# One ordered transfer queue and residues formed by TensorE in a retention + gMLP kernel

## The chip, the cores and the metric

The kernel runs on one core of a Trainium2 chip, as one launch. The metric is the device time in microseconds of one execution; runs are given by their median. Inside a profile, times count from the first instruction, and the span is what lies between the first and the last. PE is TensorE, DVE is VectorE, ACT is ScalarE, POOL is GpSimd, SP is SyncE. "ACT's queue" and "SP's queue" are the DMA queues on which these two engines issue transfers.

## The reference

Two stages on float32 inputs. Retention: batch 4, 8 heads, 768 positions, head width 64, with a state per head that decays by `gamma`. Its output `x` (4, 768, 512) goes through a gated MLP with a matmul over the positions:

```python
for t in range(S):
    state = gamma[None, :, None, None] * state + np.einsum('bhd,bhe->bhde', k[:, :, t], v[:, :, t])
    y[:, :, t] = scale * np.einsum('bhd,bhde->bhe', q[:, :, t], state)
...
h = np.maximum(x @ w_in, 0.0)                      # 512 -> 1024
u, v = (h[..., :d_ff // 2], h[..., d_ff // 2:])
mu = np.mean(v, axis=-1, keepdims=True)
var = np.mean((v - mu) ** 2, axis=-1, keepdims=True)
v_n = (v - mu) / np.sqrt(var + 1e-06)
v_s = np.einsum('ts,bsd->btd', w_spatial, v_n) + b_spatial[None, :, None]   # 768 x 768
gated = u * v_s
return (gated @ w_out).astype(np.float32)          # 512 -> 512
```

The four weights arrive as float64 (`w_in`, `w_out`) or float32 (`w_spatial`).

## The kernel before

**Pairs.** TensorE's fast type here is `F32R`. To keep float32 accuracy, each operand of the MLP is kept as a pair, a high part (a cast to `F32R`) and a low part (the residue, whole minus high), and a product is three matmuls (`split3`, through `mm` at L110): high x high, high x low, low x high. Low parts are made by `residue` (L118), a subtraction on VectorE or POOL. The products of retention are plain float32.

**Retention.** 24 groups of 128 positions, six to a batch. `load_group(g)` brings `qv` (two transfers of 256 KB), `kk` (512 KB) and `qd` (256 KB) on SP's queue (L115), and POOL multiplies the two halves of the values in `qv` by a decay (L214). `ret_set(g)` makes scores for group g+1 and the update of the state of group g: 32 + 32 small matmuls, called `s`, whose results VectorE adds to the state (L250) or masks (L257). `ret_out(g)` makes `x`: 16 matmuls on PE, a multiplication by `qd` on VectorE into `xf` (L283), a cast on ACT into `xh` (L286) and a residue on POOL into `xl`.

**MLP.** `mlp_v(b, c)` is 12 matmuls into `v`, relu on ACT into `vr` (L320), statistics on VectorE (L321, L322) and three tiny steps on POOL that give `rs` and `nb` (L323 to L326). `mlp_norm` normalises on ACT (L332), casts to `vnh` (L333) and forms `vnl`. `item(b, i)` is one of eight pieces to a batch: `u` (12 matmuls, relu into `ur` at L354), `sp`, the spatial matmul (18 matmuls), the gate on VectorE, ACT and POOL, and `o`, 9 matmuls with `w_out`.

**Weights.** `w_in` (its v half as `winv`, its u half as `winu`) and `w_out` come as 12 raw blocks of 512 KB. `load_double(i)` loads one; `split_double(i)` makes the pair from the words of the float64: absolute value on ACT (L154), five integer and scaling steps on VectorE (L155 to L159) that leave the float32 value in `df` and a small rest in `da`, a cast on ACT into the high part (L160), the residue `df` minus high, and an addition of `da` on POOL that stores the low part (L162). The residue of blocks 0 to 3 is on VectorE, of the others on POOL. `load_spatial` brings the spatial weight in pieces (`wst`), and `split_spatial(c, half)` makes a 128 x 384 pair: a cast on ACT (L187) and a residue, 11 of 12 on VectorE, one on POOL. Raw blocks, the spatial weight and the bias `b_sp` all go on ACT's queue.

**Order.** The program text is written as words: S, X, G, L, C (split_double), K (load_spatial), W (split_spatial), V, N, I, O as above, U and Z for `ret_set` without scores or without the update. Four strings hold them: START (everything of batch 0 up to its norms), FIRST (items of batch 0 beside retention of batch 1), REST and LAST. From this text a scheduler sets the order of the instructions on each engine, by its own estimate of time; transfers keep the order of the text, and so do matmuls behind START (`pinned`). Each engine then runs its own list strictly in order, and so does each queue's issuer: an instruction that waits for a semaphore holds all that are behind it. Tiles come from pools with a number of buffers; a transfer into a buffer waits until the last reader of what was in it is done. `qv`, `kk` and `qd` have 3 buffers each, raw blocks from the sixth on have 2.

Of the kernel before, what the change touches and what calls it, by code (L numbers as in the profile page):

```python
# [26 lines left out]


START = (
    "v m L0 G0 L1 L2 L3 G1 C0 C1 S-1 G2 L4 L5 C2 S0 X0 C3 S1 X1 G3 V0 C4 S2 X2 V1 C5 G4 K0 S3 X3 "  # L30
    "N0 V2 K2 N1 V3 G5 S4 X4 N2 K4 K5 V4 N3 B U5 X5 N4 V5 L6 L7 W00 W10 W20 N5 W30 W40 W50"
)
FIRST = (
    "C6 I0 G6 C7 L8 W01 C8 L9 I1 G7 W11 W21 Z5 C9 L10 I2 S6 W31 G8 C10 L11 I3 X6 S7 W41 W51 G9 C11 "
    "I4 X7 S8 G10 I5 X8 S9 G11 I6 X9 S10 G12 V0 V1 I7 X10 S11 N0 V2 N1 V3 N2 G13 X11 V4 N3 V5 N4 O7 "
    "N5"
)
# [4 lines left out]
LAST = "I0 I1 I2 I3 I4 I5 I6 I7 O7"  # L42


BLOCKS = [0, 1, 2, 3, 4, 5, 6, 8, 7, 9, 10, 11]
VECTOR_BLOCKS = 4
VECTOR_SPATIAL = 11
WARM_UP = 10
QD_BUFS = 3


@with_exitstack
def tile_retention_gmlp(
# [7 lines left out]
    w_out: bass.AP,  # L61
    b_sp: bass.AP,
    mask: bass.AP,
    vdecay: bass.AP,
    qdecay: bass.AP,
    out: bass.AP,
):
    nc = tc.nc
    P = 128
    B = out.shape[0]  # L70
    NG = kk.shape[0]
    NC = NG // B
# [12 lines left out]
    wpool = ctx.enter_context(tc.tile_pool(name="weights", bufs=1))  # L85
    rpool = ctx.enter_context(tc.tile_pool(name="ret", bufs=2))
    mpool = ctx.enter_context(tc.tile_pool(name="mlp", bufs=2))
    ps_r = ctx.enter_context(tc.tile_pool(name="ps_r", bufs=3, space=bass.MemoryType.PSUM))
    ps_m = ctx.enter_context(tc.tile_pool(name="ps_m", bufs=2, space=bass.MemoryType.PSUM))
    ps_o = ctx.enter_context(tc.tile_pool(name="ps_o", bufs=3, space=bass.MemoryType.PSUM))  # L90

    mask_t = wpool.tile([P, C], F32, name="mask_t")
    vd_t = wpool.tile([P, NC, 2, NP], F32, name="vd_t")
    bsp_t = wpool.tile([P, S], F32, name="bsp_t")
    mhalf = wpool.tile([P, 1], F32, name="mhalf")
# [6 lines left out]
    wsp_h = wpool.tile([P, NC, S], F32R, name="wsp_h")  # L102
    wsp_l = wpool.tile([P, NC, S], F32R, name="wsp_l")
# [5 lines left out]
    def mm(out, lhs, rhs, start, stop, pin=False):  # L109
        ins = nc.tensor.matmul(out, lhs, rhs, start=start, stop=stop)  # L110
        if pin or pinned:
            tc.keep_in_program_order(ins)

    def load(dst, src):
        tc.keep_in_program_order(nc.sync.dma_start(dst, src))  # L115

    def residue(eng, out, whole, high):
        eng.tensor_tensor(out, whole, high.bitcast(F32), ALU.subtract)  # L118

    def pick(on_vector):  # L120
        return nc.vector if on_vector else nc.gpsimd

    doubles = [
        (w[:, k, 0], w[:, k, 1], src[:, k])
        for w, src in ((winv_w, w_inv), (winu_w, w_inu), (wout_w, w_out))
        for k in range(KT)
    ]
    doubles = [doubles[i] for i in BLOCKS]
    raws = {}

    def load_weight(dst, src):
        tc.keep_in_program_order(nc.scalar.dma_start(dst, src))

    def load_double(i):

        if i >= len(doubles):
            return
        if i < 6:
            tag = ("vnh", "vnl")[i // 3]
            if i % 3 == 0:  # L140
                raws[tag] = mpool.tile([P, 3, DM], I64, tag=tag, name=f"raw{i}", bufs=1)
            raws[i] = raws[tag][:, i % 3]
        else:
            raws[i] = mpool.tile([P, DM], I64, tag="raw", name=f"raw{i}")[:, :]
        load_weight(raws[i], doubles[i][2])

    def split_double(i):
        hi, lo, _ = doubles[i]
        parts = raws.pop(i).bitcast(I32).rearrange("p (n w) -> p n w", w=2)
        low, top = parts[:, :, 0], parts[:, :, 1]  # L150
        a = rpool.tile([P, DM], F32, tag="xf", name=f"da{i}")
        f = mpool.tile([P, DM], F32, tag="u", name=f"df{i}", bufs=3)
        ai, fi = a[:, :].bitcast(I32), f[:, :].bitcast(I32)
        nc.scalar.activation(a, top.bitcast(F32), AF.Abs)  # L154
# [7 lines left out]
        nc.gpsimd.tensor_tensor(lo, f, a, ALU.add)  # L162

    staged = {}

    def load_spatial(c):


        if c < 4:
            if c % 2 == 0:  # L170
                tag = ("xh", "xl")[c // 2]
                t = mpool.tile([P, 2, S], F32, tag=tag, name=f"wst{c}", bufs=3)
                load_weight(t, w_sp[:, c : c + 2])
                for i in range(2):
                    for half in range(2):
                        staged[c + i, half] = t[:, i, half * HALF : half * HALF + HALF]
        elif c < NC:
            for half in range(2):
                tag = ("t", "gh" if half else "gl")[c - 4]
                t = mpool.tile([P, HALF], F32, tag=tag, name=f"wst{c}_{half}")  # L180
                load_weight(t, w_sp[:, c, half * HALF : half * HALF + HALF])
                staged[c, half] = t[:, :]

    def split_spatial(c, half):
        cols = slice(half * HALF, half * HALF + HALF)
        whole = staged.pop((c, half))
        nc.scalar.copy(wsp_h[:, c, cols], whole)  # L187
        residue(pick(c + NC * half < VECTOR_SPATIAL), wsp_l[:, c, cols], whole, wsp_h[:, c, cols])

    queries = {}  # L190
    keys = {}
# [5 lines left out]
    def load_group(g):  # L197
        if g >= NG:
            return

        t = rpool.tile([P, 4, 2, NP, C], F32, tag="qv", name=f"qv{g}", bufs=3)
        kt = rpool.tile([P, 2, 2, NP, C], F32, tag="kk", name=f"kk{g}", bufs=3)
        qd = rpool.tile([P, NP, P], F32, tag="qd", name=f"qd{g}", bufs=QD_BUFS)
        for r in range(2):
            rows = t[ROWS[r], 2 * r : 2 * r + 2]
            load(rows.rearrange("p s i h c -> p (s i h c)"), qv[g, r])
        load(kt[:, :, :, :, :].rearrange("p s i h c -> p (s i h c)"), kk[g])
        load(qd, qdecay[g % NC])
        queries[g], keys[g], naturals[g] = (t[:, 2], t[:, 1]), kt[:, 0], kt[:, 1]
        values[g], decays[g] = (t[:, 0], t[:, 3]), qd  # L210
        for r in range(2):
            vd = vd_t[ROWS[r], g % NC].unsqueeze(3).broadcast_to([D, 2, NP, D])
            w = values[g][r][ROWS[r]]
            nc.gpsimd.tensor_tensor(w, w, vd, ALU.mult)  # L214
# [114 lines left out]
    def mlp_norm(b, c):  # L329
        vh, vl = vn[b]  # L330
        v, nb, rs = norm.pop((b, c))
        nc.scalar.activation(v, v, AF.Identity, bias=nb, scale=rs)  # L332
        nc.scalar.copy(vh[:, c], v)  # L333
        residue(nc.vector, vl[:, c], v, vh[:, c])

    gate = {}
    us = {}
# [72 lines left out]
    def item(b, i):  # L410
# [23 lines left out]
        "v": lambda b, g, n: load(vd_t, vdecay),  # L434
        "B": lambda b, g, n: load_weight(bsp_t, b_sp),
    }

    def emit(text, b, g0):
# [85 lines left out]
```

## Time and profile before

| | |
|---|---|
| median of 3 runs | 439.87 us (438.54 to 441.08) |
| profiled execution | 439.42 us |
| its span | 437.6 us |
| mean granted TensorE clock | 0.938 |
| PE busy | 383.7 us, 88% of the span |
| VectorE, POOL, ACT busy | 218.2, 174.7, 128.7 us |
| transfers | 47.44 MB in all; SP's queue 37.81 MB, ACT's 9.05 MB |

The profile's rows read as follows. A row of a timeline is: start, duration, engine, line, operation, written tile <- read tiles, shape, and in brackets how long the engine stood idle before it and what released it. A group of instructions is: count, then busy time, mean of one in ns, then idle time of the engine just before them. A row of waits is: who waited for whom, us in total, how many times, the longest. Several matmuls in one row overlap, so a single duration there is a little longer than its share. A float32 matmul stands as two records, an `F32R` matmul as one.

### The profile page before, as it was taken

The numbers are of one execution on the slowest core, as the hardware profiler recorded it, in microseconds if no ns is written. First come the engines' busy times: TensorE is split into PE (matmuls) and PEld (weight loads), VectorE is DVE, ScalarE is ACT, GpSimd is POOL, SyncE is SP. The second block draws the span as 40 slices with busy tenths as digits, with TensorE's granted clock in tenths as the row PEclk, the third lists the DMA queues.
The fourth block names the chain that finished last, engine by engine and source line by source line (L and its number), as shares of the span: only waits on it lengthen the run. The fifth ranks groups of instructions, "written<-read, shape, count | busy, mean of one in ns | idle before, by whom it ended". The sixth has DMA issues, their size and how long they took to land.

```text
span 437.6 us, 9093 instructions
## 1 busy us (share of the span) xinstructions
PE 383.7 (88%) x3786; PEld 338.0 (77%) x3786; DVE 218.2 (50%) x420; ACT 128.7 (29%) x231; POOL 174.7 (40%) x201
## 2 busy tenths in 40 slices
PE   3278964888897999999995799999999999999996
PEld 1156652787786988799994788898999988999995
DVE  4699995468775555455552223354554124322122
ACT  3122534433222114542112013451113124511212
POOL 1666765564544444634442222424352223211110
PEclk8588686889998999999999799999999999999999
DMA  8974659511244542164434500064441000100102
GB/s 245 284 246 122 195 191 272 173 48 54 94 121 124 158 154 61 63 193 121 146 99 148 166 0 1 0 191 124 124 121 73 0 1 0 73 0 1 73 0 73
DMA packets 17417, 47.44 MB, mean 108 GB/s; under 512 B 2528, under 2 KB 3296, under 8 KB 17376
## 3 DMA queue, kind: packets, MB, share of 16 engines
q1 hardware_dynamic: 14640, 37.81, 28.6%
q10 hardware_dynamic: 2736, 9.05, 6.7%
q8 instruction: 30, 0.49, 0.5%
q14 instruction: 11, 0.09, 0.1%
HBM read 40.56 MB, written 6.29 MB: 107 GB/s over the span
## 4 chain that ended last, share of the span: by engine, by line
PE 75%; DMA 9%; DVE 7%; POOL 3%; issue 2%; ACT 2%; SPq 1%; POOLq 0%; DVEq 0%; ACTq 0%
PE sp L110 21%; PE v L110 15%; PE o L110 14%; PE u L110 14%; PE s L110 6%; PE x L110 5%; DMA qv<-in_qv_dram 3%; DMA qd<-in_qdecay_dram 2%; DMA raw<-in_w_inu_dram 2%; DVE qv L257 1%; DMA kk<-in_kk_dram 1%; DVE df L157 1%; DMA raw<-in_w_out_dram 1%; POOL xl L118 1%; DVE qv L250 1%
## 5 line engine op out<-in xcount | busy, mean ns | idle before, releaser
L214 POOL TENSOR_TENSOR qv<-qv,vd_t 64x512 f32<-64x512 f32 x48 | 54.3, 1132 | 57.1 <-DMA qv<-in_qv_dram 49.8
L118 POOL TENSOR_TENSOR gl<-t,gh 128x384 fp32r<-128x384 f32 x31 | 31.5, 1016 | 111.5 <-ACT gh L380 110.4
L110 PE MATMUL u<-xh,winu_w 128*128 128x384 f32 x256 | 72.6, 347 | 1.9 <-POOL winu_w L162 1.9
L110 PE MATMUL sp<-wsp_h,vnh 128*128 128x384 f32 x192 | 64.9, 338 | 3.2 <-ACT ur L354 3.2
L110 PE MATMUL v<-winv_w,xh 128*128 128x512 f32 x192 | 65.4, 423 | 0.9 <-POOL winv_w L162 0.7
L110 PE MATMUL o<-wout_w,gh 128*128 128x512 f32 x192 | 61.1, 398 | 5.0 <-POOL wout_w L162 5.0
L110 PE MATMUL sp<-wsp_h,vnl 128*128 128x384 f32 x192 | 64.9, 338 | 0.0
L110 PE MATMUL sp<-wsp_l,vnh 128*128 128x384 f32 x192 | 64.9, 338 | 0.0
L378 DVE TENSOR_TENSOR t<-sp,bsp_t 128x384 f32<-128x384 f32 (+1 forms) x34 | 18.0, 534 | 90.9 <-PE sp L110 90.8
L110 PEld LDWEIGHTS u<-xh,winu_w 128*128 128x128 f32 x256 | 47.3, 190 | 3.9 <-POOL winu_w L162 2.3
L110 PE MATMUL s<-qv,kk 64*64 64x64 f32 x1440 | 31.5, 233 | 17.6 <-DMA kk<-in_kk_dram 13.2
L110 PEld LDWEIGHTS v<-winv_w,xh 128*128 128x128 f32 x192 | 38.8, 206 | 9.8 <-POOL winv_w L162 0.8
L110 PE MATMUL v<-winv_w,xl 128*128 128x512 f32 x96 | 40.7, 424 | 5.7 <-POOL xl L118 5.7
L110 PEld LDWEIGHTS o<-wout_w,gh 128*128 128x128 f32 x192 | 36.0, 189 | 11.6 <-POOL wout_w L162 5.8
L110 PEld LDWEIGHTS s<-qv,kk 64*64 64x64 f32 x1440 | 27.7, 144 | 21.5 <-issue 19.4
L380 ACT CAST gh<-t 128x384 fp32r<-128x384 f32 (+1 forms) x34 | 16.6, 493 | 92.5 <-DVE t L379 90.1
L257 DVE TENSOR_TENSOR qv<-s,mask_t 64x256 f32<-64x256 f32 x92 | 38.6, 420 | 10.1 <-PE s L110 8.7
L110 PE MATMUL u<-xl,winu_w 128*128 128x384 f32 x128 | 43.3, 338 | 0.0
L118 POOL TENSOR_TENSOR xl<-xf,xh 128x512 fp32r<-128x512 f32 x24 | 31.3, 1303 | 29.7 <-ACT xh L286 29.7
L110 PEld LDWEIGHTS x<-qv 128*64 128x64 f32 (+1 forms) x768 | 27.9, 146 | 16.5 <-DVE qv L250 8.3
L110 PEld LDWEIGHTS sp<-wsp_h,vnh 128*128 128x128 f32 x192 | 36.6, 191 | 3.6 <-ACT ur L354 3.5
L110 PE MATMUL x<-qv 128*64 128x64 f32 (+1 forms) x768 | 32.9, 236 | 6.4 <-DVE qv L250 6.1
(57 smaller groups left out, 525.9 us busy)
## 6 DMA issues: line engine op xcount, KB each, us to landing
qv<-in_qv_dram SPq DMA_DIRECT2D x48, 256.0 KB, 4.3
kk<-in_kk_dram SPq DMA_DIRECT2D x24, 512.0 KB, 5.6
qd<-in_qdecay_dram SPq DMA_DIRECT2D x24, 256.0 KB, 5.5
out_dram<-ot SPq DMA_DIRECT2D x23, 256.0 KB, 2.0
raw<-in_w_inv_dram ACTq DMA_DIRECT2D x4, 512.0 KB, 6.9
raw<-in_w_inu_dram ACTq DMA_DIRECT2D x4, 512.0 KB, 7.0
raw<-in_w_out_dram ACTq DMA_DIRECT2D x4, 512.0 KB, 3.8
wst<-in_w_sp_dram ACTq DMA_DIRECT2D x2, 768.0 KB, 6.2
```

Of the source, the lines that this page charges most:

```text
L110: ins = nc.tensor.matmul(out, lhs, rhs, start=start, stop=stop)
L118: eng.tensor_tensor(out, whole, high.bitcast(F32), ALU.subtract)
L157: nc.vector.scalar_tensor_tensor(fi, top, -0x40000000, ai, ALU.bitwise_and, ALU.bitwise_or)
L214: nc.gpsimd.tensor_tensor(w, w, vd, ALU.mult)
L250: nc.vector.tensor_tensor(dst, u, w[r][ROWS[1 - r], i], ALU.add)
L257: nc.vector.tensor_tensor(m[r][ROWS[r], i], ts[i][col, 0], mk, ALU.mult)
L378: nc.vector.tensor_tensor(t[:, c], pp[:, c], bsp_t[:, tc_], ALU.add)
L380: nc.scalar.copy(gh[:, c], t[:, c])
```

## The change

Four things change.

1. The raw blocks 0 to 8, the spatial weight, the bias and a new 128 x 128 float32 unit matrix `eye` go on SP's queue, in one order with the groups. Only blocks 9 to 11 stay on ACT's queue.
2. A new function `residue_unit` forms a residue on PE: one or two matmuls with the unit matrix in float32 put the whole into PSUM (for a weight block, `df` and `da`, which replaces POOL's addition too), one `F32R` matmul with minus the unit matrix takes the high part off, and ACT copies the result out of PSUM as the low part. It is used for blocks 0 to 3, six of the 12 spatial pieces and the six norm tiles of batch 0. The other six spatial residues are all on VectorE.
3. Raw blocks get 3 buffers instead of 2; `kk` and `qd` get 2 instead of 3.
4. START and FIRST are written in another order, so that group 6 and block 8 are loaded within START.

```diff
 START = (
-    "v m L0 G0 L1 L2 L3 G1 C0 C1 S-1 G2 L4 L5 C2 S0 X0 C3 S1 X1 G3 V0 C4 S2 X2 V1 C5 G4 K0 S3 X3 "
-    "N0 V2 K2 N1 V3 G5 S4 X4 N2 K4 K5 V4 N3 B U5 X5 N4 V5 L6 L7 W00 W10 W20 N5 W30 W40 W50"
+    "v m e L0 G0 C0 L1 L2 S-1 C1 G1 L3 C2 S0 X0 G2 C3 L4 L5 S1 X1 K0 V0 C4 G3 S2 X2 K2 V1 C5 N0 G4 L6 "
+    "S3 X3 V2 N1 G5 W00 W10 K4 K5 S4 X4 V3 N2 W20 W30 B V4 N3 L7 U5 X5 W40 W50 N4 V5 G6 N5 L8"
 )
 FIRST = (
-    "C6 I0 G6 C7 L8 W01 C8 L9 I1 G7 W11 W21 Z5 C9 L10 I2 S6 W31 G8 C10 L11 I3 X6 S7 W41 W51 G9 C11 "
+    "C6 L9 I0 C7 W01 L10 C8 I1 G7 W11 W21 Z5 L11 C9 I2 S6 W31 G8 C10 I3 X6 S7 W41 W51 G9 C11 "
     "I4 X7 S8 G10 I5 X8 S9 G11 I6 X9 S10 G12 V0 V1 I7 X10 S11 N0 V2 N1 V3 N2 G13 X11 V4 N3 V5 N4 O7 "
     "N5"
 )
...
-VECTOR_BLOCKS = 4
-VECTOR_SPATIAL = 11
+FIRST_QUEUE = 9
+UNIT_BLOCKS = 4
+UNIT_SPATIAL = 6
+UNIT_NORM = 6
+RAW_BUFS = 3
+KK_BUFS = 2
 WARM_UP = 10
-QD_BUFS = 3
+QD_BUFS = 2
...
+    def load_eye():
+        load(eye_t, eye)
+        nc.scalar.mul(minus_t, eye_t, -1.0)
+
+    def residue_unit(out, high, name, *parts):
+
+        n = out.shape[-1]
+        ps = ps_o.tile([P, DM], F32, tag="o", name=f"ru{name}")
+        for k, part in enumerate(parts):
+            mm(ps[:, :n], eye_t, part, start=(k == 0), stop=False)
+        mm(ps[:, :n], minus_t, high, start=False, stop=True)
+        nc.scalar.copy(out, ps[:, :n])
...
-            raws[i] = mpool.tile([P, DM], I64, tag="raw", name=f"raw{i}")[:, :]
-        load_weight(raws[i], doubles[i][2])
+            raws[i] = mpool.tile([P, DM], I64, tag="raw", name=f"raw{i}", bufs=RAW_BUFS)[:, :]
+        (load if i < FIRST_QUEUE else load_weight)(raws[i], doubles[i][2])
...
-        residue(pick(i < VECTOR_BLOCKS), f, f, hi)
-        nc.gpsimd.tensor_tensor(lo, f, a, ALU.add)
+        if i < UNIT_BLOCKS:
+            residue_unit(lo, hi, f"d{i}", f, a)
+        else:
+            residue(nc.gpsimd, f, f, hi)
+            nc.gpsimd.tensor_tensor(lo, f, a, ALU.add)
...
-                load_weight(t, w_sp[:, c : c + 2])
+                load(t, w_sp[:, c : c + 2])
...
-        residue(pick(c + NC * half < VECTOR_SPATIAL), wsp_l[:, c, cols], whole, wsp_h[:, c, cols])
+        if c + NC * half < UNIT_SPATIAL:
+            residue_unit(wsp_l[:, c, cols], wsp_h[:, c, cols], f"w{c}_{half}", whole)
+        else:
+            residue(nc.vector, wsp_l[:, c, cols], whole, wsp_h[:, c, cols])
...
-        kt = rpool.tile([P, 2, 2, NP, C], F32, tag="kk", name=f"kk{g}", bufs=3)
+        kt = rpool.tile([P, 2, 2, NP, C], F32, tag="kk", name=f"kk{g}", bufs=KK_BUFS)
...
-        residue(nc.vector, vl[:, c], v, vh[:, c])
+        if b * NC + c < UNIT_NORM:
+            residue_unit(vl[:, c], vh[:, c], f"n{b}_{c}", v)
+        else:
+            residue(nc.vector, vl[:, c], v, vh[:, c])
```

The scheduler gives the engines new orders in START. In the listings below, a row is line, operation, written tile <- read tiles, shape; numbers behind a tile's name count tiles. `raw3` is the buffer of blocks 3 to 5, `wst0` the first half of the spatial weight.

On SP, from the group 2 loads on. Before:

```order
L115 DMA qv2_166<-in_qv_dram 64x1024 x2
L115 DMA kk2_167<-in_kk_dram 128x1024
L115 DMA qd2_168<-in_qdecay_dram 128x512
L115 DMA qv3_327<-in_qv_dram 64x1024 x2
L115 DMA kk3_328<-in_kk_dram 128x1024
L115 DMA qd3_329<-in_qdecay_dram 128x512
```

After:

```order
L123 DMA qv2_255<-in_qv_dram 64x1024 x2
L123 DMA kk2_256<-in_kk_dram 128x1024
L123 DMA qd2_257<-in_qdecay_dram 128x512
L123 DMA raw3_174<-in_w_inu_dram 128x512 x2
L123 DMA wst0_343<-in_w_sp_dram 128x1536
L123 DMA qv3_382<-in_qv_dram 64x1024 x2
L123 DMA kk3_383<-in_kk_dram 128x1024
L123 DMA qd3_384<-in_qdecay_dram 128x512
L123 DMA wst2_454<-in_w_sp_dram 128x1536
L123 DMA qv4_497<-in_qv_dram 64x1024 x2
```

Weight blocks 4 and 5 and the spatial weight now stand between the groups, behind `qd2` and `qd3`; `qd2` goes into the buffer that `qd0` had, `qd3` into that of `qd1`.

On VectorE, around `xf1`, the last step of group 1's `x`. Before:

```order
L257 TENSOR_TENSOR qv2_166<-s1_1_265,mask_t_73 64x256 x2
L283 TENSOR_TENSOR xf1_323<-x1_306,qd1_115 128x512
L155 TENSOR_SCALAR da4_362<-da4_362 128x512
L321 BN_STATS bst0_0_352<-vr0_0_351 128x6
L156 TENSOR_SCALAR da4_362<-da4_362 128x512
```

After:

```order
L284 TENSOR_TENSOR qv2_255<-s1_1_281,mask_t_73 64x256 x2
L126 TENSOR_TENSOR wsp_l_83<-wst0_343,wsp_h_82 128x384 x2
L310 TENSOR_TENSOR xf1_339<-x1_322,qd1_167 128x512
L176 TENSOR_SCALAR da4_371<-da4_371 128x512
L177 TENSOR_SCALAR da4_371<-da4_371 128x512
```

Two spatial residues, which read `wst0`, have moved ahead of `xf1`.

On PE, at the end of START. Before:

```order
L110 MATMUL v0_5_750<-winv_w_78,xh3_541 128x512 x2
L110 MATMUL v0_5_750<-winv_w_78,xl3_542 128x512
L110 MATMUL u0_0_0_804<-xh0_247,winu_w_79 128x384
L110 MATMUL u0_0_0_804<-xl0_248,winu_w_79 128x384
L110 MATMUL u0_0_0_804<-xh0_247,winu_w_79 128x384 x2
```

After:

```order
L118 MATMUL v0_5_815<-winv_w_80,xh3_567 128x512 x2
L118 MATMUL v0_5_815<-winv_w_80,xl3_568 128x512
L118 MATMUL run0_4_811<-vr0_4_747,eye_t_74 128x512
L118 MATMUL run0_4_811<-vnh0_345,minus_t_75 128x512
L118 MATMUL run0_5_850<-vr0_5_828,eye_t_74 128x512
L118 MATMUL run0_5_850<-vnh0_345,minus_t_75 128x512
L118 MATMUL u0_0_0_869<-xh0_249,winu_w_81 128x384
L118 MATMUL u0_0_0_869<-xl0_250,winu_w_81 128x384
```

The unit matmuls of norm tiles 4 and 5 (`run0_4`, `run0_5`) now stand between the last `v` and the first `u`; the one of tile 5 reads the tile that ACT normalises after `nb5`.

More of the change, by code (lines that the diff above doesn't have):

```diff
@@ L63, in tile_retention_gmlp @@
     mask: bass.AP,
+    eye: bass.AP,
     vdecay: bass.AP,
@@ L92, in tile_retention_gmlp @@
     mask_t = wpool.tile([P, C], F32, name="mask_t")
+    eye_t = wpool.tile([P, P], F32, name="eye_t")
+    minus_t = wpool.tile([P, P], F32R, name="minus_t")
     vd_t = wpool.tile([P, NC, 2, NP], F32, name="vd_t")
@@ L180, in load_spatial @@
                 t = mpool.tile([P, HALF], F32, tag=tag, name=f"wst{c}_{half}")
-                load_weight(t, w_sp[:, c, half * HALF : half * HALF + HALF])
+                load(t, w_sp[:, c, half * HALF : half * HALF + HALF])
                 staged[c, half] = t[:, :]
@@ L434, in tile_retention_gmlp @@
         "v": lambda b, g, n: load(vd_t, vdecay),
-        "B": lambda b, g, n: load_weight(bsp_t, b_sp),
+        "e": lambda b, g, n: load_eye(),
+        "B": lambda b, g, n: load(bsp_t, b_sp),
     }
@@ L503 @@
         "mask": np.concatenate([causal, causal]),
+        "eye": np.eye(P, dtype=np.float32),
         "vdecay": vdecay.astype(np.float32),
```

## The prediction

> **What bounds the kernel now.** I read the stages first. The columns are us, each engine's busy time with its instructions, the granted TensorE clock, the DMA share and GB/s.
>
> ```profile
> 0.00:81.70 81.70, 50.16 (x642) 36.95 (x643) 62.35 (x110) 26.53 (x46) 48.58 (x53) 0.75 0.74 219
> ...
> 140.00:437.60 297.60, 285.39 (x2657) 257.79 (x2655) 116.74 (x246) 82.93 (x150) 98.92 (x125) 0.99 0.26 81
> ```
>
> From 140 us on PE is busy 96% and the change leaves those stages as they are. All that can be won lies ahead of 140: START, which ends where the first `u` begins (81.77), with PE busy 50 of 82 us, and the first items behind it. So I asked what PE waits for from 60 to 140 us, and where START's end and the first `sp` tile's end stand on PE:
>
> ```profile
> PE v L110 <- POOL xl L118: 5.1, 1, 5.1
> PE o L110 <- POOL wout_w L162: 5.0, 2, 3.4
> PE sp L110 <- ACT ur L354: 3.2, 1, 3.2
> PE u L110 <- POOL winu_w L162: 1.9, 1, 1.9
> ...
> 81.77 0.34 PE L110 MATMUL u<-xh,winu_w 128*128 128x384 f32 x1
> ...
> 94.10 0.34 PE L110 MATMUL u<-xh,winu_w 128*128 128x384 f32 x1
> ```
>
> The `winu_w` and `wout_w` waits are for weight blocks that come or are split late. Then the transfers, since the change is mostly one of transfer order: two stretches with the queues full, one between them, and a weight block that went through an empty queue.
>
> ```profile
> 6.00:24.00 18.00, 4.49 (x114) 4.06 (x116) 13.61 (x24) 3.92 (x7) 9.27 (x7) 0.56 1.03 289
> 20.00:70.00 50.00, 36.49 (x574) 28.05 (x574) 47.73 (x88) 17.51 (x32) 30.03 (x30) 0.81 0.66 196
> 238.00:246.00 8.00, 2.84 (x51) 2.76 (x52) 0.97 (x3) 0.00 (x0) 3.06 (x4) 0.65 1.03 277
> ...
> 100.52 3.81 DMA raw<-in_w_out_dram
> ```
>
> Full queues move 277 to 289 GB/s, and I take 0.285 MB per us. In 238 to 246 only SP's queue had work, so one queue is as fast as two. A block of 0.524 MB needs 1.84 us at that rate and took 3.81, so 2.0 us is the fixed part of a transfer issued into an empty queue. From 20 to 70 us the queues ran at 66%: SP stood still while it waited for buffers. Whom SP waits for, and two rows of VectorE that free them:
>
> ```profile
> SPq L115 <- DVE qv L250: 84.7, 14, 44.0
> SPq L115 <- PE x L110: 63.3, 15, 9.4
> ...
> 26.03 0.69 DVE L283 TENSOR_TENSOR xf<-x,qd 128x512 f32<-128x512 f32 x1
> ...
> 35.49 0.69 DVE L283 TENSOR_TENSOR xf<-x,qd 128x512 f32<-128x512 f32 x1
> ```
>
> These are `xf0` and `xf1`. Before, such a wait held up retention groups only; the weights had ACT's queue. Afterwards blocks 4 to 8 and the spatial weight stand behind the groups on SP, and with two `qd` buffers `qd2` waits for `xf0`, `qd3` for `xf1`, and so on. That is the new coupling, and the sum turns on it.
>
> **The residues.** Removed from VectorE are 4 block residues, 5 spatial and 6 norm residues, from POOL 4 block additions and one spatial residue:
>
> ```profile
> L118 DVE TENSOR_TENSOR df<-df,winv_w 128x512 f32<-128x512 f32 x4 | 4.4, 1109 | 0.0
> L118 DVE TENSOR_TENSOR wsp_l<-wst,wsp_h 128x384 fp32r<-128x384 f32 x11 | 7.0, 654 | 5.3 <-ACT wsp_h L187 5.2
> L118 DVE TENSOR_TENSOR vnl<-vr,vnh 128x512 fp32r<-128x512 f32 x24 | 18.3, 765 | 13.9 <-ACT vnh L333 13.9
> L162 POOL TENSOR_TENSOR winv_w<-df,da 128x512 fp32r<-128x512 f32 x4 | 5.3, 1342 | 0.2
> L187 ACT CAST wsp_h<-wst 128x384 fp32r<-128x384 f32 x12 | 5.5, 507 | 5.7 <-DMA wst<-in_w_sp_dram 5.7
> L320 ACT ACTIVATE vr<-v 128x512 f32<-128x512 f32 x24 | 14.3, 597 | 45.3 <-PE v L110 45.2
> ```
>
> VectorE loses 4 x 1.109 + 5 x 0.654 + 6 x 0.765 = 12.3 us and POOL 4 x 1.342 + 1.0 = 6.4 us. ACT gains 16 copies out of PSUM, 10 at 0.60 (as `vr<-v`) and 6 at 0.51 (as the 384-wide cast): 9 us, on an engine busy 26.5 of 81.7. PE gains 20 matmuls with the f32 unit matrix and 16 f32r ones. The trace has no f32 matmul 512 wide. Its bounds are two rows:
>
> ```profile
> 224.94 1.15 PE L110 MATMUL x<-qv 128*64 128x64 f32 x32
> ...
> 117.21 3.12 PE sp L110 x18
> ```
>
> In the first, 16 f32 products of 64 columns, two abreast, are 512 columns in 1.15 us (each product stands as two records). In the second an f32r matmul of 384 columns takes 0.173, so 512 would take 0.23. I take 1.15 (0.86 for 384 columns), since it is f32, and 0.23 for the f32r part; the low end would save 0.9 per unit matmul. In all, 14 x 1.15 + 6 x 0.86 + 3.4 = 25 us of PE in START. Most lies in PE's 31 idle us there; what does not is counted below.
>
> **The chain through SP.** Its further prices:
>
> ```profile
> L214 POOL TENSOR_TENSOR qv<-qv,vd_t 64x512 f32<-64x512 f32 x48 | 54.3, 1132 | 57.1 <-DMA qv<-in_qv_dram 49.8 <-DVE wsp_l L118 5.2 <-PE u L110 0.7
> L332 ACT ACTIVATE vr<-vr,nb,rs 128x512 f32<-128x512 f32 x24 | 19.4, 810 | 5.7 <-POOL nb L326 5.7
> ```
>
> By the same view `rs`, its power and `nb` on POOL are together 1.2 us, and an instruction of VectorE in START's middle is 47.73 / 88 = 0.54 us (20 to 70 above).
>
> 1. `xf0` ends at 26.7, as before: START's head (the first blocks, two groups, S0) is bound by the same bytes. `qd2`, blocks 4 and 5 and the first half of the spatial weight follow in one piece, 2.10 MB: 7.4 + 2.0, so `wst0` lands at 36.1.
> 2. Two spatial residues of `wst0` now stand ahead of `xf1` on VectorE, and wait for ACT's casts. Casts 2.0, residues 0.6 (as little as 0.56 each where undisturbed, the first beside the casts), `xf1` 0.7: it ends at 39.4, where before it ended at 36.2.
> 3. `qd3`, the second spatial piece and `qv4` are 1.57 MB: `qv4` lands at 46.9.
> 4. POOL multiplies it ahead of `nb0`, which comes at 49.3. (The first half lands 0.9 earlier, and `rs0`'s power is between the halves.) Norm 0 (0.8) and the first step of block 5 (0.6) follow on ACT, then VectorE in its order, 13 instructions of 0.54, half a group of `x` on PE (0.6) and `xf3` (0.7). PE meanwhile stands at the unit matmul of tile 0, in the middle of S3, and with it the scores that VectorE needs. `xf3` ends at 59.0.
> 5. `qd5`, four spatial pieces, the bias, block 7, `qv6`: 2.48 MB, 8.7 + 2.0. `qv6` lands at 69.7.
> 6. POOL's second half of `qv6`, then `rs3`, power, `nb3`, then ACT's norm 3: 1.13 + 1.2 + 0.8, so 72.9.
> 7. PE waits there with tile 3's unit matmul, ahead of `v4` and most of `x5`. That pair (1.4), two spatial pairs (2.1), twelve `v4` matmuls (2.8) and the rest of `x5` (0.6) are 6.8 us at full clock, some 7.3 with the first part slow. With `xf5` itself, 80.9.
> 8. `qd7` waits for `xf5`, and `qv8` is behind it: 0.79 MB, 2.8 + 2.0, landing at 85.7. POOL has `qv8` ahead of `nb4`, then the last two steps of block 6, then `nb5`: 1.1 + 2.7 + 1.2, so 90.7. Norm 5 (0.8) and the unit pair of tile 5 at half clock (2.7): the first `u` starts at 94.2.
> 9. Two `u` tiles are 24 matmuls of 0.173, 4.2, and 1.7 more while the clock is still low; `sp` 3.1: the first `sp` ends at 103.2, against 94.10. That is **+9.1**. The 3.2 us wait for `ur` falls away in it, because ACT is free by then.
> 10. Behind it the three waits for weights, 5.0 + 1.9 = 6.9 us, go: blocks 7 and 8 land in START, and three raw buffers let 9 to 11 start early. In their place POOL holds block 11's addition behind the landing of `qv9`, 2.4 us at the fourth `o` (a transfer's fixed part plus a bit; between 0 and 4.8, a landing behind 0.79 MB). That is **-4.5**.
>
> What else moves costs nothing by these rows: POOL and VectorE are off PE's path after 140 us (busy 99 and 117 of 298), and two `kk` buffers instead of three mean that a group's keys start one item later than before, (437.6 - 81.8) / 32 = 11 us, and need 5.6 (the page's time to landing). The worst wait behind 140 stays:
>
> ```profile
> 243.16 1.97 PE L110 MATMUL s<-qv,kk 64*64 64x64 f32 x48 [7.42 <-DMA kk<-in_kk_dram]
> ```
>
> The sum is +4.6 on the profiled execution's own 439.4 us, so **444.0**; the median shown is 439.9, 0.5 above that execution.
>
> **The clock, and a page against it.** Where PE had waited 5.1 us, its next matmuls were twice as long:
>
> ```profile
> 73.76 0.80 PE L110 MATMUL v<-winv_w,xl 128*128 128x512 f32 x1 [5.12 <-POOL xl L118]
> ...
> 73.70:75.70 2.00, 1.94 (x5) 1.56 (x6) 0.47 (x1) 0.80 (x2) 1.73 (x5) 0.50 1.07 237
> ```
>
> For the 2 us behind that wait the granted clock was 0.50. So the waits in steps 6 and 8 are paid twice, in the wait and in some 2 us after it; both steps hold that. The Trainium skill ("TensorE: Matmul & The Clock Gate", Part 1: The HAM clock gate) says that one idle window of about 3.4 us puts the array to half clock. The rows agree, and by the rule alone the unit matmuls speak against the change wherever they wait for a norm.
>
> **Rivals.** *Faster: SP does not stall.* If the `xf` instructions keep pace with the transfers, all that is between `qd2` and `qv8` (12.7 MB) flows at 0.285: 44.6 us from 26.7, plus 2.0, `qv8` lands at 73 and by step 8 the first `u` is at 81.5, the first `sp` ends at 89, and with step 10 the time is 439.4 - 5 - 4.5 = 430. For it: VectorE is busiest in START (62 of 82) and loses 12 us. Also for it, two instructions of one form and line:
>
> ```profile
> 10.04 0.68 DVE L118 TENSOR_TENSOR df<-df,winv_w 128x512 f32<-128x512 f32 x1
> ...
> 12.44 1.53 DVE L118 TENSOR_TENSOR df<-df,winv_w 128x512 f32<-128x512 f32 x1
> ```
>
> The second ran beside POOL and took 0.85 longer; 15 such instructions gone can give POOL and the rest of VectorE back up to 15 x 0.85 = 13 us. The Trainium skill ("SBUF — State Buffer", Who interferes with whom) says why: VectorE with two SBUF inputs and GpSimd reading SBUF share one port, and the loser blocks. The rows agree. Against it: the `xf` are also held by PE and POOL in order (steps 2, 4, 7), and from 20 to 70 us even two queues with three buffers ran at 196 GB/s; by that rate `qv8` would land at 26.7 + 65 = 92, later than mine. Chance 0.30.
>
> *No change.* Either the unit matmul is near the f32r price, which takes 0.9 from tile 3, 1.4 from the spatial pairs and 1.8 (at half clock) from tile 5; or `xf0` comes 4.4 earlier because VectorE is rid of four residues of 1.1. Each alone shifts the chain by 4.1 to 4.4, the first `u` to about 90. Then 439.4 + 9.1 - 4.3 - 4.5 = 439.7. For it: both are single unknowns with an end there. Against it: by the column the f32 products of `x` are five times as dear as f32r, and `xf0` also waits for S0. Chance 0.20.
>
> *Slower still: half-depth prefetch bites later.* If two buffers make a wait like the 7.42 us at 243 once more, on top of my sum: 451. Against it, PE is 96% busy there with SP waiting for `x` and `qv`, not for `kk`. Chance 0.12.
>
> **How the numbers follow.** My forecast has 0.38, its own range 441 to 448 (unit matmuls at a middle price below; above, 4.8 instead of 2.4 in step 10 and 1.7 more of half clock). The range of 429 to 451 takes in the other cases' times and leaves out the tails of the outer two, together some 0.2. No change can be told within 0.5%, 2.2 us. Slower holds my forecast and the last rival, 0.50; within, 0.20; faster, 0.30.
>
> **What would show it.** After the change: the first half of the spatial weight landing near 36, `xf1` near 39, `xf3` near 59, `qv8` near 86, the first `u` near 94; SP waiting for VectorE's `xf`; PE waiting at the unit matmuls for ACT's `vr`; no wait for `winu_w` or `wout_w` between 95 and 140. I am wrong if `xf` runs ahead of the transfers (DMA share near 1 from 27 to 70 us), or if the f32 unit matmul is not near 1.15.

## The result and the profile after

The changed kernel takes 458.39 us (457.4 to 459.62), the kernel before 439.21 in the same runs: 4.3% slower, a ratio of 1.0428 (1.0385 to 1.0471). The forecast of 444.0 had the sign; the time lies above its range. In two of the variants below, `mulpin` and `oldres_qdlate`, two and three of the ten runs were slower than the others and are left out of the times (with them the medians are 439.59 and 434.29). The profiled execution has a span of 456.8 us, with the first `u` at 107.64.

The stages, with the columns as before: START, the first items, the rest.

```profile
0.00:107.60 107.60, 75.10 (x698) 44.33 (x699) 59.06 (x111) 39.78 (x71) 45.04 (x53) 0.82 0.63 179
107.60:140.00 32.40, 32.40 (x255) 30.61 (x254) 19.79 (x31) 9.03 (x18) 14.01 (x11) 0.95 0.16 50
140.00:456.80 316.80, 300.40 (x2892) 270.31 (x2890) 129.22 (x263) 88.02 (x160) 106.69 (x132) 0.98 0.28 84
```

START is 26 us longer. From 107.6 to 140 PE is busy without a gap, so the `winu_w` and `wout_w` waits of the kernel before are gone there, as step 10 had it. What PE waits for from 60 to 140 us, and SP's largest wait for a load over the whole run:

```profile
PE run L118 <- ACT vr L359: 10.8, 3, 4.7
PE v L118 <- ACT xh L313: 1.5, 1, 1.5
...
SPq L123 <- DVE xf L310: 130.2, 17, 11.4
```

`run` is the unit matmul of a norm tile, `vr` the tile that ACT normalises. Three places hold it up, for tiles 3, 4 and 5. On PE's timeline around them:

```profile
82.38 2.08 PE L118 MATMUL run<-vr,eye_t 128*128 128x512 f32 x2 [4.00 <-ACT vr L359]
...
91.34 0.33 PE L118 MATMUL x<-qv 128*64 128x64 f32 x2
...
99.26 1.12 PE L118 MATMUL run<-vr,eye_t 128*128 128x512 f32 x2 [2.12 <-ACT vr L359]
...
105.34 2.08 PE L118 MATMUL run<-vr,eye_t 128*128 128x512 f32 x2 [4.72 <-ACT vr L359]
106.43 1.42 PE L118 MATMUL run<-vnh,minus_t 128*128 128x512 f32 x1
107.64 0.52 PE L118 MATMUL u<-xh,winu_w 128*128 128x384 f32 x1
```

The pair of records `x2` is one f32 matmul: 1.12 us at a granted clock of 1.00 (99.2 to 100.5 us), 2.08 at 0.50 (105.3 to 107.6). The last two records of `x5` are at 91.34, behind tile 3's unit matmul and all of `v4`, and `xf5` follows at 91.76. On POOL, what stands ahead of `nb3` and of `nb4` and `nb5`:

```profile
77.86 1.03 POOL L241 TENSOR_TENSOR qv<-qv,vd_t 64x512 f32<-64x512 f32 x1 [8.15 <-PE s L118]
79.12 1.04 POOL L241 TENSOR_TENSOR qv<-qv,vd_t 64x512 f32<-64x512 f32 x1 [0.23 <-DMA qv<-in_qv_dram]
80.26 0.21 POOL L350 TENSOR_SCALAR rs<-mv 128x1 f32<-128x1 f32 x1
80.56 0.56 POOL L351 TENSOR_TENSOR rs<-rs,mhalf 128x1 f32<-128x1 f32 x1
81.22 0.26 POOL L353 TENSOR_SCALAR nb<-mv,rs 128x1 f32<-128x1 f32 x1
...
96.78 1.17 POOL L241 TENSOR_TENSOR qv<-qv,vd_t 64x512 f32<-64x512 f32 x1 [0.76 <-DMA qv<-in_qv_dram]
97.93 0.43 POOL L353 TENSOR_SCALAR nb<-mv,rs 128x1 f32<-128x1 f32 x1
98.44 1.04 POOL L241 TENSOR_TENSOR qv<-qv,vd_t 64x512 f32<-64x512 f32 x1
99.56 1.27 POOL L126 TENSOR_TENSOR df<-df,winu_w 128x512 f32<-128x512 f32 x1
100.92 1.26 POOL L186 TENSOR_TENSOR winu_w<-df,da 128x512 fp32r<-128x512 f32 x1
...
103.46 0.98 POOL L353 TENSOR_SCALAR nb<-mv,rs 128x1 f32<-128x1 f32 x1
```

POOL stood idle for 8 us until `qv6` could be multiplied (the row of its second half, at 79.12, names the landing), and `nb3` came only behind that; tile 3's norm, PE's unit matmul, `x5`, `xf5` and with it SP's next transfer, `qd7` with `qv8` behind it, followed in turn. Then POOL had the first half of `qv8` ahead of `nb4`, and its second half and block 6 ahead of `nb5`.

### The profile page after: what moved, and what is told of

The parts are those of the page before. It is cut to its first block, busy times and chain, and to the rows that moved or that the text cites. A ratio compares the mean times of both kernels' runs of the same rounds, so it can differ in the third digit from the quotient of the medians.

```text
span 456.8 us, 9204 instructions
## 1 busy us (share of the span) xinstructions
PE 407.9 (89%) x3842; PEld 345.2 (76%) x3842; DVE 208.1 (46%) x405; ACT 136.8 (30%) x248; POOL 165.7 (36%) x196
## 4 chain that ended last, share of the span: by engine, by line
PE 71%; DMA 12%; DVE 5%; POOL 4%; issue 3%; SPq 2%; ACT 2%; POOLq 0%; DVEq 0%; ACTq 0%
PE sp L118 21%; PE u L118 16%; PE o L118 14%; PE v L118 9%; DMA qv<-in_qv_dram 6%; PE s L118 5%; PE x L118 4%; SPq L123 2%; DMA wst<-in_w_sp_dram 2%; DMA raw<-in_w_inv_dram 2%; PE run L118 2%; POOL qv L241 1%; DMA kk<-in_kk_dram 1%; ACT vr L359 1%; DVE xf L310 1%
## 5 line engine op out<-in xcount | busy, mean ns | idle before, releaser
L241 POOL TENSOR_TENSOR qv<-qv,vd_t 64x512 f32<-64x512 f32 x48 | 51.9, 1080 | 86.4 <-DMA qv<-in_qv_dram 76.0
L118 PE MATMUL u<-xh,winu_w 128*128 128x384 f32 x256 | 73.8, 352 | 0.0
L118 PE MATMUL v<-winv_w,xh 128*128 128x512 f32 x192 | 62.3, 405 | 3.7 <-ACT xh L313 2.8
L118 PEld LDWEIGHTS u<-xh,winu_w 128*128 128x128 f32 x256 | 48.6, 195 | 2.1 <-issue 0.5
L118 PEld LDWEIGHTS v<-winv_w,xh 128*128 128x128 f32 x192 | 36.2, 192 | 12.6 <-ACT xh L313 3.3
L284 DVE TENSOR_TENSOR qv<-s,mask_t 64x256 f32<-64x256 f32 x92 | 38.6, 420 | 10.7 <-PE s L118 9.6
L118 PE MATMUL v<-winv_w,xl 128*128 128x512 f32 x96 | 38.1, 397 | 1.5 <-POOL xl L126 1.5
L277 DVE TENSOR_TENSOR qv<-s,qv 64x256 f32<-64x256 f32 x80 | 33.8, 422 | 10.0 <-PE s L118 4.3
L118 PE MATMUL o<-wout_w,gl 128*128 128x512 f32 x96 | 38.2, 398 | 0.0
L118 PEld LDWEIGHTS x<-qv 128*64 128x64 f32 (+1 forms) x768 | 27.6, 142 | 13.8 <-issue 10.2
```

The lines of the kernel that those rows point to most:

```text
L277: nc.vector.tensor_tensor(dst, u, w[r][ROWS[1 - r], i], ALU.add)
L284: nc.vector.tensor_tensor(m[r][ROWS[r], i], ts[i][col, 0], mk, ALU.mult)
```

## The experiments

Times are medians; ratios, where given, are to the kernel before in the same runs. With every edit the scheduler sets the orders of the engines anew, so small moves besides the intended one can occur. In the cuts of the code, `...` stands for lines left out. The first four ask which part of the change costs: theory Q (the one queue and its wait for `xf`, on which the prediction was built), rival U (PE standing at unit matmuls) and rival B (two buffers instead of three).

**qdlate.** `load_qd(g)` loads `qd` of group g; it is called in `load_group(g + 1)`, behind that group's `qv` and `kk`.

```diff
+    def load_qd(g):
+        qd = rpool.tile([P, NP, P], F32, tag="qd", name=f"qd{g}", bufs=QD_BUFS)
+        load(qd, qdecay[g % NC])
+        decays[g] = qd
...
-        load(qd, qdecay[g % NC])
+        if g - 1 in queries and g - 1 not in decays:
+            load_qd(g - 1)
...
```

> The changed kernel, with one edit: the transfer of qd(g) is issued behind the qv and kk of group g+1 instead of its own, so that SP no longer waits for xf(g-2) ahead of the weights; buffers, residues and engine orders nearly as in the changed kernel. Theory Q (the coupling of the one queue: weights and later groups stand on SP behind a wait for xf): the second spatial half and qv4, issued at 42.5 and 43.1 us now, are issued near 33, the first u starts at 92 to 97 instead of 107.6, and the time falls by 10 to 15 us to 443 to 448. Rival U (PE stands at the unit matmuls of the norm tiles, whatever the transfers do): the first u moves by under 3 us, 455 or more. Rival B (two buffers of kk and qd cost by themselves, also behind START): no more than half of the 19 us comes back, 449 to 455.

452.05 us. Some 6 of the 19 us come back, and the first `u` moves from 107.6 to 103.6. SP's wait for `xf` is a cost, and not the main one: less comes back than theory Q asks (443 to 448), more than rival U allows (455 or more). The time would fit rival B (449 to 455), which `oldres` below sets aside: 441.05 with the same two buffers.

**twoqueues.**

```diff
-FIRST_QUEUE = 9
+FIRST_QUEUE = 0
-                load(t, w_sp[:, c : c + 2])
+                load_weight(t, w_sp[:, c : c + 2])
...
```

> The changed kernel with all raw weight blocks, the spatial weight and the bias on ACT's queue as before; START, buffers and unit residues as changed. Theory Q: weights land early again, wst0 before 30 us, xf1 before 38, the first u by 93, time 438 to 446. Rival U: the waits at the unit matmuls stay and hold x and v, 452 or more. Rival B: 448 to 455.

454.81 us. Theory Q's figure is missed: with the weights on their own queue again 3.6 of the 19.2 us come back and the rest of the loss stays. Rivals U and B both allow this time.

**oldres.**

```diff
-UNIT_BLOCKS = 4
-UNIT_SPATIAL = 6
-UNIT_NORM = 6
+UNIT_BLOCKS = 0
+UNIT_SPATIAL = 0
+UNIT_NORM = 0
...
-            residue(nc.gpsimd, f, f, hi)
+            residue(pick(i < 4), f, f, hi)
...
-            residue(nc.vector, wsp_l[:, c, cols], whole, wsp_h[:, c, cols])
+            residue(pick(c + NC * half < 11), wsp_l[:, c, cols], whole, wsp_h[:, c, cols])
```

> The changed kernel with the residues as before (VectorE and POOL, none on PE), one queue, two buffers and the new START kept. Theory Q: the queue still waits for xf, and four spatial residues instead of two now stand ahead of xf1; first u near 105, time 453 to 462. Rival U: the PE waits at unit matmuls are gone and most of the loss with them, 439 to 446. Rival B: 450 to 458.

441.05 us, a ratio of 1.0037 (1.0004 to 1.007): what rival U has, and neither Q nor B. The residues are worth 17.3 us, with the queue, the buffers and START left as changed. The `xf` instructions start at nearly the times of the changed kernel up to `xf4` (75.0 against 76.7), so the transfers were as late; but `xf5` starts at 78.0 instead of 91.8. On PE's timeline the first `u`, and the first place that waits for a late norm:

```profile
87.38 0.33 PE L118 MATMUL u<-xh,winu_w 128*128 128x384 f32 x1
...
96.65 0.69 PE L118 MATMUL sp<-wsp_h,vnh 128*128 128x384 f32 x1 [2.84 <-ACT vnh L360]
```

With the low part formed on VectorE nothing on PE stands for norms 4 and 5 until the last third of the first `sp`: two `u` tiles and 12 of 18 `sp` matmuls run first.

**nonorm.**

```diff
-UNIT_NORM = 6
+UNIT_NORM = 0
```

> The changed kernel with only the six norm residues back on VectorE; blocks and spatial pieces still by unit matmuls. Theory Q: the 11.7 us of PE waits for vr at the unit matmuls turn into other waits for the same transfers, first u 100 to 106, time 450 to 457. Rival U: they are the loss, 443 to 448. Rival B: as theory Q, 450 to 458.

446.17 us: the six norm residues are 12.2 of the 17.3 us, blocks and spatial pieces the other 5.1. The first four runs bear out rival U, with some 6 us for the wait for `xf` beside it.

The next four ask what the unit matmuls cost: a loop through POOL and SP (theory L) or their PE time (rival P).

**mulpin.** POOL's multiplication of a group's values moves from `load_group(g)` to `ret_set(g - 1)`, and it and `nb` keep the order of the text.

```diff
+    def multiply(g):
         for r in range(2):
             vd = vd_t[ROWS[r], g % NC].unsqueeze(3).broadcast_to([D, 2, NP, D])
             w = values[g][r][ROWS[r]]
-            nc.gpsimd.tensor_tensor(w, w, vd, ALU.mult)
+            tc.keep_in_program_order(nc.gpsimd.tensor_tensor(w, w, vd, ALU.mult))
...
+        if nxt:
+            multiply(g + 1)
...
-        nc.gpsimd.tensor_scalar(nb, mv[:, 0:1], rs, -1.0, ALU.mult, ALU.mult)
+        tc.keep_in_program_order(
+            nc.gpsimd.tensor_scalar(nb, mv[:, 0:1], rs, -1.0, ALU.mult, ALU.mult)
+        )
```

> The changed kernel with POOL's multiplication of a group's values put off until the scores of that group, and kept there with nb in the order of the text: nb3 to nb5 no longer stand behind the landing of qv6 to qv8. Queue, buffers, unit residues and PE's order as changed. Theory L (a loop: transfer, POOL's multiplication, nb, the norm, PE's unit matmul in front of x, xf, SP's next transfer): the waits of unit matmuls for vr fall from 11.7 to under 3 us, the first u starts near 93 instead of 107.6, time 442 to 448. Rival P (the price of the f32 unit matmuls on PE, with the low clock): the matmuls are as dear as ever, 453 or more.

439.1 us, all of the loss, with every unit matmul kept; a larger gain than theory L had (442 to 448), though the waits for `vr` fell to 5.3 us and not to under 3. POOL's timeline at `nb3` and PE's waits from 60 to 140 us:

```profile
72.90 0.21 POOL L354 TENSOR_SCALAR rs<-mv 128x1 f32<-128x1 f32 x1 [5.63 <-DVE mv L353]
73.20 0.57 POOL L355 TENSOR_TENSOR rs<-rs,mhalf 128x1 f32<-128x1 f32 x1
73.86 0.27 POOL L358 TENSOR_SCALAR nb<-mv,rs 128x1 f32<-128x1 f32 x1
...
PE run L118 <- ACT vr L365: 5.3, 2, 4.2
```

`nb3` now follows its statistics at once, 7.4 us earlier, and the first `u` starts at 93.5. That is 14 of the 20 us between the two profiled executions; the other 6 lie behind the first `u`, where the order is pinned too, and were not followed up. PE's order moved as well: all of `x5` stands ahead of `v4` here, so not all of the gain need be POOL's alone.

**late3.**

```diff
+        if c == 5 and late:
+            residue_unit(*late.pop())
...
-            residue_unit(vl[:, c], vh[:, c], f"n{b}_{c}", v)
+            if c == 3:
+                late.append((vl[:, c], vh[:, c], f"n{b}_{c}", v))
+            else:
+                residue_unit(vl[:, c], vh[:, c], f"n{b}_{c}", v)
```

> The changed kernel with the unit residue of norm tile 3 emitted behind V5, so that on PE it stands behind v5 and not ahead of v4 and x5; nothing else moves on purpose. Theory L: xf5 ends near 80 instead of 92.5, qv8 lands near 86 instead of 97, the first u starts at 97 to 100, time 447 to 451. Rival P: one matmul pair has only changed its place, 456 or more.

453.85 us, between the two expectations. Tile 3's place is worth 4.5 us. `xf5` did start early, at 84.29, but the first `u` only at 106.03: POOL still had `qv7`, `qv8` and block 6 ahead of `xl` and the last `nb`, and PE waited for these instead:

```profile
PE v L118 <- POOL xl L126: 4.3, 1, 4.3
PE run L118 <- ACT vr L363: 4.1, 1, 4.1
```

**cheap.** The high part stands in for the whole, so the low parts are left out (they come out as zero).

```diff
+    plus_t = wpool.tile([P, P], F32R, name="plus_t")
...
+        nc.scalar.copy(plus_t, eye_t)
...
-            mm(ps[:, :n], eye_t, part, start=(k == 0), stop=False)
+            mm(ps[:, :n], plus_t, high, start=(k == 0), stop=False)
```

> The changed kernel with the unit matmuls in the fast type: the high part instead of the whole is multiplied, so the low parts come out as zero. A 512-wide unit matmul then costs 0.23 us instead of 1.1. The scheduler then also sets tile 3's pair behind v5, as in the run before. Theory L: what the place brings plus a few unit matmuls on the path, 445 to 450. Rival P: 25 us of PE time are gone, and with them nearly all of the loss, 438 to 443.

444.58 us, between the two expectations: 13.8 us come back, of which tile 3's place is 4.5 by `late3`. Price and place went together here, since the scheduler moved tile 3's pair; the run doesn't part them, so up to 9 us may be price. `mulpin_cheap` below parts them for the pinned order.

**oldres_qdlate**, the edits of `oldres` and `qdlate` together.

> No unit residues at all, one queue, two buffers, the new START, and qd(g) behind the qv and kk of group g+1. With the loop through PE gone (441.05 without the last edit) the wait for xf on SP is what is left of the coupling: theory L expects 435 to 440, a few us from the earlier landings of the spatial weight and qv4; if SP's wait for xf costs nothing once the loop is open, 440 to 442.

433.6 us, 0.9856 (0.9814 to 0.9898): faster than before, a little more so than theory L had (435 to 440). With the residues as before the wait for `xf` costs 7.5 us.

**oldres_mulpin**, the edits of `oldres` and `mulpin` together.

> Both edits that each brought the 19 us back, together: residues as before, and nb of POOL not behind the multiplications. Theory L (the unit matmuls and POOL's order make one loop, so that opening it at either place is enough): the second edit brings little once the first is made, 435 to 441. Rival C (two separate costs, about 17 us for the residues and 19 for POOL's order, that add): 420 to 426.

429.01 us, 0.9726 (0.967 to 0.9781), the fastest of all; it lies between the two theories. The four runs make a table:

| | POOL's order as scheduled | POOL's order pinned |
|---|---|---|
| unit residues | 458.39 | 439.1 |
| residues as before | 441.05 | 429.01 |

The residues cost 17.3 us with the scheduled order and 10.1 with the pinned one, POOL's order 19.3 and 12.0. Only 7.2 us are of the kind that theory L means, where opening the loop at either place is enough; the rest are two costs that add.

**before_mulpin**, the edit of `mulpin` in the kernel before.

> The kernel before with POOL's order pinned in the same way. Theory L: there is no loop to open, so within 4 us of the kernel before, 436 to 443. Rival C: POOL's order costs the kernel before as much, 420 to 425.

449.92 us, 1.0202 (1.0133 to 1.0271): slower, which neither theory had. The pinned order suits the new START and not the old one. Ahead of the first `u` PE waits 9.3 us for `xh` in this run, against 0.2 in the kernel before, and behind it 5.1 us for `winu_w`, against 1.9; why was not followed up.

**before_onequeue.**

```diff
-        load_weight(raws[i], doubles[i][2])
+        (load if i < 9 else load_weight)(raws[i], doubles[i][2])
...
-                load_weight(t, w_sp[:, c : c + 2])
+                load(t, w_sp[:, c : c + 2])
...
```

> The kernel before with one edit: weight blocks 0 to 8, the spatial weight and the bias on SP's queue in the order of the old START; three buffers, old residues. The prediction's own chain gave the coupling through one queue the whole of its +9.1 us: if it holds by itself, 445 to 450. Theory L: without the unit matmuls on PE the norms hold no x, so the queue has slack, 438 to 444.

439.02 us, 0.9971 (0.994 to 1.0002). One queue by itself costs nothing. This clears the queue and not the coupling, since with three `qd` buffers SP shows no wait for `xf` to speak of in this run.

**mulpin_qdlate**, the edits of `mulpin` and `qdlate` in the changed kernel.

> The changed kernel whole, with unit residues, plus the pinned order on POOL and qd(g) behind the qv and kk of group g+1. Theory L: with the loop open on POOL the late wait for xf brings what it brought without unit residues (441.05 to 434.3), so 431 to 437. If the wait for xf costs nothing here, 438 to 441.

439.81 us, within noise the same as `mulpin`: here the wait for `xf` is hidden, and theory L's figure (431 to 437) was missed.

The last four ask what the 10.1 us are that unit residues cost under the pinned order: the place of tiles 4 and 5 in front of `u` (theory P2) or the price (rival P).

**mulpin_norm4**, `mulpin` with one number changed; PE's order in START is that of `mulpin` without the four matmuls in front of the first `u`.

```diff
-UNIT_NORM = 6
+UNIT_NORM = 4
```

> The kernel with POOL's order pinned (439.6), and the residues of norm tiles 4 and 5 alone back on VectorE; on PE nothing else moves, the four unit matmuls in front of the first u are gone. Theory P2 (place: PE stands there for the last norms while u and most of sp could run): the first u starts near 82 to 84 instead of 93.5, time 429 to 433. Rival P (price: what is left of the residues' cost is their PE time, spread over START): two of 16 residues, under 3 us, 437 to 440.

432.1 us, 0.9813 (0.9775 to 0.9852): 7.0 us for two residues. PE goes from the last `v` into the first `u`:

```profile
83.85 0.40 PE L118 MATMUL v<-winv_w,xh 128*128 128x512 f32 x1
...
85.22 0.33 PE L118 MATMUL u<-xh,winu_w 128*128 128x384 f32 x1
```

In `mulpin` PE stood there for 4.2 us, and its four unit matmuls took another 4.4 at a granted clock of 0.50 (89.0 to 93.5 us):

```profile
89.10 2.08 PE L118 MATMUL run<-vr,eye_t 128*128 128x512 f32 x2 [4.17 <-ACT vr L365]
...
93.53 0.50 PE L118 MATMUL u<-xh,winu_w 128*128 128x384 f32 x1
```

**mulpin_norm0**, `mulpin` with `UNIT_NORM = 0`.

> POOL's order pinned and all six norm residues back on VectorE; four weight blocks and six spatial pieces still by unit matmuls. Theory P2: as the run before, or up to 3 us more for the waits at tiles 0 to 3, 427 to 433. Rival P: 6 of 16 residues, 435 to 438.

435.7 us, slower than with four tiles on PE, so P2's figure was missed and rival P's (435 to 438) was met. For tiles 0 to 3 VectorE is not the better place under this order; the reason stays open. Against `oldres_mulpin` the run leaves 6.7 of the 10.1 us with the block and spatial residues, and no run takes these apart.

**mulpin_cheap**, the edits of `mulpin` and `cheap` together.

> POOL's order pinned and the unit matmuls in the fast type (the low parts come out as zero), places on PE much as in the pinned kernel, but tile 3's pair behind v5. Theory P2: the place in front of u is kept, so PE still stands there, 435 to 439. Rival P: 25 us of PE time gone, 428 to 432.

438.05 us, 0.9933 (0.9903 to 0.9963), as P2 has it: the cheap matmul brings 1.1 us where `mulpin_norm4` brought 7.0. PE still stands in front of `u`, for tile 4 here and again for tile 5:

```profile
85.74 0.50 PE L119 MATMUL run<-vnh,plus_t 128*128 128x512 f32 x1 [3.56 <-ACT vnh L368]
...
89.75 0.52 PE L119 MATMUL u<-xh,winu_w 128*128 128x384 f32 x1
```

The first `u` starts 3.8 us earlier than in `mulpin`, but the first `u` matmuls now run at the low clock (granted 0.50 from 88.7 to 93.2; 0.52 us a row where `mulpin_norm4` has 0.33), so the first `sp` ends only 2.0 us earlier. For tiles 4 and 5 under the pinned order it is the place far more than the price.

**mulpin_oldres_qdlate**, three edits together.

> The three edits that brought time back, together: no unit residues, POOL's order pinned, qd(g) behind the qv and kk of group g+1. If the wait for xf on SP still costs what it did without the pinned order (441.05 to 434.3), 421 to 426; if it is hidden now, as it was with unit residues and the pinned order (439.6 to 439.8), 428 to 430.

435.08 us: 6 us slower than `oldres_mulpin`, where both expectations had it as fast or faster. The edit of `qdlate` brought 6.3 us on the changed kernel, 7.5 on `oldres`, nothing on `mulpin`, and loses 6.1 here. In this run `xf0` and `xf1` start earlier than in `oldres_mulpin` and `xf3` and `xf5` later (65.1 and 78.4 us against 62.8 and 72.9); what holds them is open.

## Why the prediction was wrong

The forecast had the sign, and the chain of its steps is, but for step 4, the one that the trace shows. It fell short of the time by 14 us, and what it made of the chain was wrong.

**The sizes.** The chain of work that ended last, in the changed kernel, with the pieces that answer to steps 1, 3, 4 and 8:

```profile
29.03 9.20 DMA wst<-in_w_sp_dram
...
43.05 8.01 DMA qv<-in_qv_dram
...
61.89 3.03 PE v L118 x10
...
92.92 3.73 DMA qv<-in_qv_dram
```

| end of | forecast | measured | late by |
|---|---|---|---|
| `xf0` | 26.7 | 27.7 | 1.0 |
| `wst0` landed | 36.1 | 38.2 | 2.1 |
| `xf1` | 39.4 | 42.1 | 2.7 |
| `nb0` | 49.3 | 54.6 | 5.3 |
| `xf3` | 59.0 | 66.3 | 7.3 |
| norm 3 | 72.9 | 82.3 | 9.4 |
| `xf5` | 80.9 | 92.5 | 11.6 |
| `nb5` | 90.7 | 104.4 | 13.7 |
| first `u` starts | 94.2 | 107.6 | 13.4 |
| first `sp` | 103.2 | 116.4 | 13.2 |

No single term makes the 13 us: five links, steps 3, 4, 5, 7 and 8, were some 2 us short each, and they add. Transfers are the largest part, some 5 us. Step 3's first half of `qv4` was to land at 46.0 and landed at 51.1, 2.4 us more than the lateness of `xf1`; from `xf3` to `qv6` step 5 had 10.7 us and the trace 12.8. The prediction counted only the bytes ahead of a transfer; those issued right behind it (`kk4`) were in flight too, which may be the reason (no run tells it apart).

Step 4 had the wrong path. It put VectorE's 13 instructions between `nb0` and `xf3`; these were done at 62.4 us, and VectorE stood idle until 65.6, because the second half of `x3` stands on PE behind nearly all of `v2` (the 3.03 us above). Step 7 had its matmuls, but took half a microsecond for the low clock where all from 82.4 to about 87 ran at it (the 2.08 us of the first; the granted clock was 0.52 from 82.3 to 87.1). The prediction had read 2 us of low clock behind the wait in the kernel before. There the low clock lasted longer:

```profile
75.70:77.70 2.00, 2.00 (x6) 1.59 (x5) 1.15 (x1) 1.75 (x4) 1.85 (x2) 0.50 0.99 308
77.70:81.70 4.00, 4.00 (x14) 3.14 (x13) 1.76 (x4) 0.60 (x1) 3.46 (x5) 0.72 0.30 116
```

Step 8 had 5.0 us from the landing of `qv8` to the end of `nb5`; POOL took 7.8.

Behind the first `sp`, step 10 was near. From its end to the end of the span are 456.8 - 116.4 = 340.4 us, before 437.6 - 94.1 = 343.5: -3.1 where -4.5 was forecast. The 2.4 us that POOL's addition was to cost at an `o` came as one wait of 2.5. The wait at 243 stayed, as 8.34 us at 263:

```profile
262.96 1.98 PE L118 MATMUL s<-qv,kk 64*64 64x64 f32 x48 [8.34 <-DMA kk<-in_kk_dram]
```

**The cause.** The prediction wrote that "the sum turns on" the coupling through SP's queue. That step failed. SP's wait for `xf` is real, but in the changed kernel it is worth 6.3 of the 19.2 us (`qdlate`). With the old residues, the queue, the buffers and the new START together, that wait included, come to 441.05, and without the wait to 433.6, so they make next to no loss. What makes the loss are the places that steps 6, 7 and 8 name in passing: POOL's `nb` behind the landing of a later group, PE's unit matmul behind `nb`, and `x5` and `u` behind the unit matmul. With the coupling kept, taking the residues off PE brings back 17.3 us (`oldres`), and pinning POOL's order 19.3 (`mulpin`). So the sign came true for a reason to which the prediction gave little weight. Had these places been set up as the coupling, one would have seen that VectorE's residue, which the change removes, is on nobody's path until the fifth of six pieces of `sp`, while the unit matmul is on PE's path at once. What stays open is why the block and spatial residues cost 5 to 7 us, and what `mulpin` gains behind the first `u`.

**The price of the unit matmul** was right: 1.12 us for 512 columns, 1.15 taken. So was the statement that its waits are paid twice through the clock: 2.08 us behind waits of 4.0 and 4.72 us, 1.12 behind one of 2.12. The length of the wait alone does not tell, though: in `oldres` the clock was 0.50 behind 2.84 us (96.6 to 99.0), in `mulpin_cheap` 1.00 behind 3.56 (85.7 to 86.5). Under the pinned order the price was not the point, as `mulpin_cheap` shows. Under the scheduled order `cheap` gave 444.58, not the 439.7 of the rival "no change", which rested on the price, and that with tile 3's pair moved.

**The faster rival** rested on `xf` keeping pace with the transfers. The trace shows the opposite: SP waits 130.2 us in all for `xf`, 42.4 of them ahead of 107.6 us, and the DMA share from 27 to 70 us is 0.63. Its other ground, VectorE's freed time, came true (59 us busy in a longer START, 62 before) and bought nothing: VectorE was not what the next step waited for. The pair of rows shown for it says less than was read from it: the first one, at 10.04, ran beside POOL too, which was busy from 10.08 to 13.42. The rival of half-depth buffers found nothing to carry it: the wait at 263 is one as before, and with the same two buffers `oldres_mulpin` runs in 429.0.

## What to carry to other kernels

Work moved from VectorE's list to PE's cost more here by its place in the order than by its PE time: everything behind it on PE now waits for its inputs, so ask what it waits for and what could have run instead. This is shown for norm tiles 4 and 5, and in part for tile 3; for the block and spatial residues it is not shown. Two in-order lists that each hold one unready instruction ahead of a ready one (POOL's landing ahead of `nb`, PE's norm ahead of `x`) feed each other through the transfers; look for such a pair before pricing either. Here pinning POOL's order, which keeps the tiny `nb` steps clear of later groups' landings, was worth 12 to 19 us with the new START, and cost the kernel before some 10, so try it anew for each order. The fastest version keeps the one queue, the new START and the shallow buffers, leaves the residues on VectorE and POOL and pins POOL: 429.0 us.

## What the runs showed of the hardware

Small instructions on POOL vary by two to nearly four in one execution: the power of `rs`, 128 x 1, took 0.56 us at 80.56 and 1.06 at 94.96, and `nb` 0.26 at 81.22 and 0.98 at 103.46.

```profile
94.96 1.06 POOL L351 TENSOR_TENSOR rs<-rs,mhalf 128x1 f32<-128x1 f32 x1
```

In front of `u` three of them in a row stand on the path, so such a stretch is seen in the end time.
